# An fp32 opening for an attention and two-MoE kernel: one product in place of three for the first 24 blocks, weights split later, and gathers of 256 rows

## The chip, the cores and the metric

The kernel runs on one NeuronCore of a Trainium2 chip. The metric is the device time of one launch in microseconds (us). Five engines work beside each other, each through its own queue in order: TensorE (PE, with its weight loads shown as PEld), VectorE (DVE), ScalarE (ACT), GpSimd (POOL) and SyncE (SP), which here only issues DMAs. [...]

## The reference, cut to what matters

```python
# 1. windowed attention, 4 x 576 tokens, 8 heads of 64, window 128, ALiBi bias
scores = q @ k.T / 8 + bias            # masked to 0 <= i - j < 128
x = softmax(scores) @ v                # -> x: 2304 tokens x 512
# 2. one dense MLP, d_ff 2048; its weights are float64
h = x @ w_in;  g = where(h > 0, h, exp(min(h, 0)) - 1);  x = g @ w_out
# 3. token routing: skip score, argmax over 8 experts, then per expert (d_ff 1024)
y = gate * (relu(x @ w1[e]) @ w2[e]);  out = x + y     # where x @ w_skip > 0
```

## The kernel before, in words

**Chunks and blocks.** The 2304 tokens go in nine chunks of 256. The dense MLP of a chunk is 16 blocks of 128 hidden columns: `P1` computes `h` for a block (lines 332 to 359) and `P2` (line 361) adds the block's share to the two output accumulators `acc`. A list `seq` (line 488) sets the order of blocks: chunk 0's blocks 0 to 7, chunk 1's 0 to 7, chunk 0's 8 to 15, chunk 1's 8 to 15, and from place 32 on chunk 2 to 8 whole. "Step `st`" below is a place in that list; P2 follows its P1 by two steps. So the weights of a half of the MLP serve two chunks before the other half is needed.

**Precision.** [...] Each operand is split into a high part (ACT copies it to fp32r) and a low part (a subtraction on DVE or POOL), and three products stand for one: P1 of a block is 12 matmuls of 256 columns, P2 is 6 of 512. The first 16 heads (`NATIVE = 2` chunks, functions `n_S` to `n_xT`) are done in plain fp32 instead, with no split; a plain fp32 matmul shows as two records in the trace. The later heads (`att_A`, `att_B`, `att_C`) are split.

**The opening** is written out by hand in lines 523 to 600: a loop over `k`, in which the instructions of PE, ACT, DVE and POOL keep the program's order. In step `k` head `k` of the first 16 is done; from `k = S0 = 10` on, step `st = k - 10` of `seq` joins. The same loop converts the 32 float64 weight tiles of the MLP (a "half" is one of the two tiles of a block; `CV` says how many per `k`) to fp32 by three integer operations on DVE: `shift` writes `wt`, `top` and `low` write `wr`. Then `cut` makes the split: ACT writes the high part of `w`, POOL (first 24) or DVE (last 8) subtracts. POOL also does the subtraction of `P1_g` while `k < 26`.

**After the loop** a scheduler orders the instructions. Heads 16 to 71 come one per step or one per two steps; the routing of a chunk follows its last P2; the third part runs expert by expert (`M1`, `M2`), where `gather` reads the tokens of an expert, `xpose` transposes them on PE, and `xcut` splits them. An expert's place holds `CAP = 192` rows, read as 128 and 64 (`NJ`). Between the last dense block and the first expert, `old_rows` (line 698) brings expert 0's earlier tokens into PSUM by a product with the identity, and the rank of the last chunk's tokens (`rt_rank`) follows it on PE.

Of the kernel before, what the change touches and what calls it, by code (L numbers as in the profile page):

```python
# [28 lines left out]
NATIVE = 2  # L29
HALF = NF1 // 2  # L30
S0 = 10
PINNED = 16
GPOOL = 26
# [27 lines left out]
def attn_moe_kernel(ctx: ExitStack, tc: tile.TileContext, a, out: bass.AP):  # L61
# [43 lines left out]
    later = []  # L105
# [21 lines left out]
    def low(f, x):  # L127
        lo, hi = (W[f][x][:, :, z] for z in range(2))
        DVE.scalar_tensor_tensor(out=lo, in0=lo, scalar=29, in1=hi, op0=ALU.logical_shift_right, op1=ALU.bitwise_or)

    def cut(f, x):
        w = wp.tile([128, 2, 512], F32R, name="w", tag="w")
        v = W[f][x][:, :, 0].bitcast(F32)
        ACT.activation(out=w[:, 0], in_=v, func=ACTF.Copy)
        W[f][x] = w
        rest = lambda: (POOL if f < LO_POOL else DVE).tensor_tensor(out=w[:, 1], in0=v, in1=w[:, 0].bitcast(F32), op=ALU.subtract)
        if f < LO_POOL:
            rest()
        else:
            later.append(rest)  # L140
# [71 lines left out]
    def n_max(i):  # L212
        u, h = divmod(i, 2)
        c, hp = divmod(u, 4)
        S = St.pop(i)
        p = p_p.tile([128, 2, 256], F32, name="p")
        m = smp.tile([128, 2], F32, name="m")
        den = smp.tile([128, 2], F32, name="den")
        for t in range(2):
            lo = 128 if (c == 0 and t == 0) else 0  # L220
            DVE.tensor_tensor_reduce(out=p[:, t, lo:], in0=S[:, t, lo:], in1=bias[:, 2 * hp + h, lo:], scale=-0.125, scalar=3e38, op0=ALU.add, op1=ALU.min, accum_out=m[:, t:t + 1])
        for t in range(2):
            lo = 128 if (c == 0 and t == 0) else 0
            ACT.activation(out=p[:, t, lo:], in_=p[:, t, lo:], func=ACTF.Exp, bias=m[:, t:t + 1], scale=-1.0, accum_out=den[:, t:t + 1])
        Pt[i] = p, den

    def n_norm(i):
# [31 lines left out]
    def n_xT(i):  # L259
# [101 lines left out]
    def P2(c, f):  # L361
# [112 lines left out]
    def init_slots():  # L474
# [7 lines left out]
        for j0, n in NJ:  # L482
            nc.sync.dma_start(out=xv[j0:j0 + n], in_=zero[0:n, None, :].to_broadcast([n, NE, RW]))
# [25 lines left out]
    rq = []  # L509
    load_bias = lambda h: nc.sync.dma_start(out=bias[:, h:h + 2].rearrange("p h n -> p (h n)"), in_=a["bias"][:, h * 256:h * 256 + 512])  # L510
# [15 lines left out]
    plan = [[todo.pop(0) for _ in range(min(n, len(todo)))] for n in CV]  # L526
    for k in range(S0 + PINNED):
# [14 lines left out]
        halves = plan[k]  # L542
        if st >= 8:
            for z in halves:
                shift(*z)
        if st >= 1:
            P1_g(*seq[st - 1], POOL if k < GPOOL else DVE)
# [10 lines left out]
        if 0 <= k - 1 < 16:
            n_T(k - 1)
        if 0 <= st < 8:  # L560
            for z in halves:
                shift(*z)
        if st < 0:
            for z in halves:
                top(*z)
        if k < 16:
            n_norm(k)
        if st >= 0:
            for z in halves[0:1]:
                top(*z)  # L570
            while later:
                later.pop()()
        else:
            for z in halves:
                low(*z)
            if st < -1:
                for z in plan[k + 1]:
                    shift(*z)
        if 0 <= k - 2 < 16:
            n_xT(k - 2)  # L580
        if st >= 0:
            for z in halves[1:2]:
                top(*z)
            for z in halves:
                low(*z)
# [5 lines left out]
        for z in halves:  # L591
            if st < 0:
                later.append(lambda z=z: cut(*z))
            else:
                cut(*z)
    while later:
        later.pop()()
# [4 lines left out]
    for i in range(16, 24):  # L602
        begin[i] = i + 5, i + 5
# [25 lines left out]
    sC = {b[1]: i - 1 for i, b in begin.items() if i > 16}  # L629
    sC[begin[NU - 1][1] + 2] = NU - 1  # L630
    for st in range(PINNED, len(seq) + 2):
        if st == PINNED:
            load_h(18)
            load_h(19)
        if st == PINNED:
            for e in (PE, ACT, DVE, POOL):
                e.on = True
            split_h(16)
            split_v(8)
            split_h(17)  # L640
            for e in (PE, ACT, DVE, POOL):
                e.on = False
# [23 lines left out]
        after_P2(*seq[st - 2])  # L666
        if st in sB:
# [255 lines left out]
```

## Time and profile before

| | us |
|---|---|
| median of 3 runs | 793.34 (792.83 to 795.66) |
| the profiled execution | 792.31 |
| its span | 790.6 |
| PE busy | 737.1 (93%) |
| DVE busy | 602.3 (76%) |
| ACT busy | 534.0 (68%) |
| POOL busy | 335.6 (42%) |

The profiled execution is a run of its own, 1.03 us under the median; the 1.7 us beside its span is launch and end. Busy shares are means over stages that have different limits, so they are read by stage. In a line of the timeline the first two numbers are start and duration; `x12` counts records merged into one line; the bracket at the end is how long the engine sat idle before and what ended that.

### The profile page before, as it was taken

To read this page: it belongs to the slowest core of one execution; us is meant where nothing else is said; L and a number is where in the kernel's file an instruction comes from. 1 tells how busy PE (TensorE), PEld (TensorE's weight loads), DVE (VectorE), ACT (ScalarE), POOL (GpSimd) and SP (SyncE) were. 2 spreads that over 40 slices of the span, in tenths; PEclk is the share of its full clock that TensorE was granted. 3 is DMA by queue.
4 is the path that set the end of the run, shared out by engine and by line. 5 is a ranking of instruction groups with operands and counts; after the bars stand their busy time and mean duration, and the time that the engine had idled before them with its cause. 6 is when DMAs were issued, how large, how long until landed. Compare 5 with 4: busy or idle time off the path is not lost.

```text
span 790.6 us, 14785 instructions
## 1 busy us (share of the span) xinstructions
PE 737.1 (93%) x4963; PEld 655.1 (83%) x4965; DVE 602.3 (76%) x1563; ACT 534.0 (68%) x1416; POOL 335.6 (42%) x350
## 2 busy tenths in 40 slices
PE   6786799989999999999999999999998999999995
PEld 3364587879999989999999999999887999998894
DVE  5999994898888888888888888875335777776772
ACT  6776466777778768778777777766444766666661
POOL 1445654344454354354344344321104565655651
PEclk9889999999999999999999999999998999999998
DMA  8866117432222222222222222105014666666630
GB/s 284 310 231 230 60 50 221 125 98 93 84 62 83 86 89 61 81 71 75 80 77 88 73 76 82 34 13 211 19 47 124 216 225 218 212 208 220 232 129 29
DMA packets 43212, 98.94 MB, mean 125 GB/s; under 512 B 7779, under 2 KB 15843, under 8 KB 43132
## 3 DMA queue, kind: packets, MB, share of 16 engines
q1 hardware_dynamic: 40092, 93.40, 36.9%
q0 software_dynamic: 3040, 4.56, 1.6%
q8 instruction: 40, 0.66, 0.3%
q14 instruction: 40, 0.33, 0.1%
HBM read 85.35 MB, written 15.93 MB: 128 GB/s over the span
## 4 chain that ended last, share of the span: by engine, by line
PE 70%; DVE 16%; ACT 5%; issue 4%; DMA 3%; SPq 0%; POOL 0%; POOLq 0%; ACTq 0%; DVEq 0%
PE h L52 23%; PE acc L52 21%; PE h L744 4%; DVE wr L52 4%; DVE wt L52 3%; PE PT L52 3%; PE S L52 3%; PE PV L52 3%; PE m L52 3%; PE acc L762 2%; ACT p L52 2%; DMA w2r<-in_w2c_dram 2%; PE h L745 2%; DVE p L52 2%; DVE den L52 2%
## 5 line engine op out<-in xcount | busy, mean ns | idle before, releaser
L52 PE MATMUL h<-xT,w 128*128 128x256 f32 x1728 | 238.6, 287 | 4.8 <-DVE e L52 2.4
L52 PEld LDWEIGHTS h<-xT,w 128*128 128x128 f32 x1728 | 221.7, 191 | 12.6 <-DVE e L52 4.7
L52 PE MATMUL acc<-w,gt 128*128 128x512 f32 x864 | 225.9, 396 | 2.2 <-POOL gt L52 2.2
L52 PEld LDWEIGHTS acc<-w,gt 128*128 128x128 f32 x864 | 154.2, 191 | 28.0 <-POOL gt L52 2.6
L52 POOL TENSOR_TENSOR w<-w2r,w 128x512 fp32r<-128x512 f32 x64 | 88.3, 1400 | 86.9 <-ACT w L52 66.0
L185 POOL TENSOR_TENSOR hi<-qkr,hi 64x256 fp32r<-64x256 f32 x56 | 41.5, 741 | 166.5 <-issue 127.0
L52 ACT ACTIVATE e<-h 128x256 f32<-128x256 f32 x144 | 55.0, 382 | 75.8 <-PE h L52 75.5
L52 DVE TENSOR_TENSOR gt<-e,gt 128x256 fp32r<-128x256 f32 x129 | 59.9, 464 | 36.5 <-ACT gt L52 35.2
L52 DVE SCALAR_TENSOR_TENSOR e<-h,e 128x256 f32<-128x256 f32 x144 | 60.6, 421 | 31.0 <-ACT e L52 30.8
L52 ACT ACTIVATE p<-p,m 128x256 f32<-128x256 f32 (+1 forms) x144 | 70.5, 490 | 13.2 <-DVE m L52 12.6
L744 PE MATMUL h<-xT,w 128*128 128x384 f32 x256 | 78.7, 364 | 0.4 <-DVE xT L736 0.4
L52 ACT ACTIVATE w<-w2r 128x512 fp32r<-128x512 f32 x128 | 74.6, 628 | 5.3 <-DMA w2r<-in_w2c_dram 5.2
L52 ACT ACTIVATE gt<-e 128x256 fp32r<-128x256 f32 x144 | 58.8, 408 | 23.5 <-DVE e L52 23.1
L186 POOL TENSOR_TENSOR kl<-qkr,hi 128x384 fp32r<-128x384 f32 x56 | 62.7, 1119 | 4.4
L745 PE MATMUL h<-xT,w 128*128 128x192 f32 x256 | 64.1, 250 | 0.0
L52 ACT ACTIVATE e<-e 128x256 f32<-128x256 f32 x144 | 60.1, 417 | 4.1
L52 PE MATMUL PT<-ident,p 128*128 128x128 f32 x280 | 48.2, 289 | 14.1 <-ACT p L52 9.4
L52 POOL TENSOR_TENSOR w<-wr,w 128x512 fp32r<-128x512 f32 x24 | 35.7, 1504 | 54.0 <-ACT w L52 51.2
L52 DVE TENSOR_TENSOR w<-w2r,w 128x512 fp32r<-128x512 f32 x64 | 53.0, 865 | 6.7 <-ACT w L52 6.7
L52 PEld LDWEIGHTS PT<-ident,p 128*128 128x128 f32 x280 | 32.6, 144 | 28.7 <-ACT p L52 16.0
L52 DVE CUSTOM_DVE_ANT_0 p<-S,bias 128x256 f32<-128x256 f32 (+1 forms) x104 | 41.2, 408 | 17.0 <-PE S L52 16.9
L762 PE MATMUL acc<-gt,w 128*128 128x384 f32 x128 | 42.7, 367 | 8.3 <-DVE yT L770 5.9
(130 smaller groups left out, 1468.3 us busy)
## 6 DMA issues: line engine op xcount, KB each, us to landing
w2r<-in_w2c_dram SPq DMA_DIRECT2D x64, 512.0 KB, 4.3
qkr<-in_qk_dram SPq DMA_DIRECT2D x112, 160.0 KB, 2.9
wr<-in_w1c_dram SPq DMA_DIRECT2D x32, 512.0 KB, 6.2
v<-in_v_dram SPq DMA_DIRECT2D x36, 192.0 KB, 2.8
out_dram<-x SPq DMA_DIRECT2D x18, 256.0 KB, 3.2
qkr<-in_qk_dram SPq DMA_DIRECT2D x8, 320.0 KB, 6.0
bsp<-in_bsp_dram SPq DMA_DIRECT2D x20, 128.0 KB, 2.1
xg<-xs SPq DMA_DIRECT2D x9, 257.0 KB, 3.9
```

The costliest lines, as they stand in the source:

```text
L52: i = op(*args, **kw)
L185: eng.tensor_tensor(out=hi[64:128, 0:256], in0=r[64:128, 0:256], in1=hi[64:128, 0:256].bitcast(F32), op=ALU.subtract)
L186: eng.tensor_tensor(out=kl, in0=r[:, 256:640], in1=hi[:, 256:640].bitcast(F32), op=ALU.subtract)
L744: nc.tensor.matmul(out=h[:, 0:2 * CAP], lhsT=w[0][:, 0, kc * 128:kc * 128 + 128], rhs=x[:, kc].rearrange("p a n -> p (a n)"), start=kc == ...
L745: nc.tensor.matmul(out=h[:, 0:CAP], lhsT=w[0][:, 1, kc * 128:kc * 128 + 128], rhs=x[:, kc, 0], start=False, stop=kc == 3)
L762: nc.tensor.matmul(out=o[:, 0:2 * CAP], lhsT=w[1][:, 0, dc * 128:dc * 128 + 128], rhs=gt.rearrange("p a n -> p (a n)"), start=f == 0, stop ...
```

## The change

The constants move the loop's start of the MLP one step forward (`S0` 10 to 9), raise `NATIVE` to 3 chunks and spread the conversions differently (`CV`). `plain` names the 24 blocks (all 16 of chunk 0 and the first 8 of chunk 1) that are computed in plain fp32: P1 with 4 matmuls, P2 with 2, and `P1_g` writes `gt` in one DVE operation. `low` now writes the fp32 weights packed into the first half of their own tile, and no split follows in the loop. The splits (`parts`, 16 of them, each two ACT copies and two DVE subtractions) are handed to the scheduler at steps 16 to 27. `xf`, an unsplit x for chunks 0 and 1, takes one of the two buffers of `xTp`; `x_parts` splits chunk 1's later.

```diff
-NATIVE = 2
+NATIVE = 3
-S0 = 10
+S0 = 9
-GPOOL = 26
-CV = [0] * 2 + [1] * 8 + [2] * 8 + [1] * 8
-LO_POOL = 12
+CV = [0] * 2 + [1] * 7 + [2, 1] * 4 + [2] * 6 + [1] + [0] * 4
+C2 = 21
...
     def low(f, x):
-        lo, hi = (W[f][x][:, :, z] for z in range(2))
-        DVE.scalar_tensor_tensor(out=lo, in0=lo, scalar=29, in1=hi, op0=ALU.logical_shift_right, op1=ALU.bitwise_or)
-
-    def cut(f, x):
-        w = wp.tile([128, 2, 512], F32R, name="w", tag="w")
-        v = W[f][x][:, :, 0].bitcast(F32)
-        ACT.activation(out=w[:, 0], in_=v, func=ACTF.Copy)
-        W[f][x] = w
-        rest = lambda: (POOL if f < LO_POOL else DVE).tensor_tensor(out=w[:, 1], in0=v, in1=w[:, 0].bitcast(F32), op=ALU.subtract)
...
+        r = W[f][x]
+        v = r.rearrange("p n two -> p (n two)")[:, 0:512]
+        DVE.scalar_tensor_tensor(out=v, in0=r[:, :, 0], scalar=29, in1=r[:, :, 1], op0=ALU.logical_shift_right, op1=ALU.bitwise_or)
+        W[f][x] = v.bitcast(F32)
+
+    def parts(f):
+        for x in range(2):
+            w = wp.tile([128, 2, 512], F32R, name="w", tag="w")
+            v = W[f][x]
+            ACT.activation(out=w[:, 0], in_=v, func=ACTF.Copy)
+            DVE.tensor_tensor(out=w[:, 1], in0=v, in1=w[:, 0].bitcast(F32), op=ALU.subtract)
+            W[f][x] = w
...
+    plain = lambda c, f: c == 0 or c == 1 and f < HALF
...
+            if plain(c, f):
+                PE.matmul(out=h[:, 0:256], lhsT=w[0][:, kc * 128:kc * 128 + 128], rhs=xf[:, c, kc], start=kc == 0, stop=kc == 3)
+                continue
...
+        if plain(c, f):
+            DVE.scalar_tensor_tensor(out=gt[:, 0], in0=h[:, 0:256], scalar=0.0, in1=e, op0=ALU.max, op1=ALU.subtract)
+            G[c, f] = gt
+            return
...
+            if plain(c, f):
+                PE.matmul(out=o, lhsT=gt[:, 0, sl], rhs=w[1], start=first, stop=final)
+                continue
...
-        for j0, n in NJ:
-            nc.sync.dma_start(out=xv[j0:j0 + n], in_=zero[0:n, None, :].to_broadcast([n, NE, RW]))
+        for j0 in (0, 128):
+            nc.sync.dma_start(out=xv[j0:j0 + 128], in_=zero[:, None, :].to_broadcast([128, NE, RW]))
...
+    ready = {}
+    for f in range(HALF):
+        ready.setdefault(16 + 2 * f // 3, []).append(f)
+        ready.setdefault(20 + f, []).append(HALF + f)
...
-        for j, (j0, n) in enumerate(NJ):
-            r0 = e * TS + j0
-            nc.sync.dma_start(out=xg[e][0:n, j], in_=xs[r0:r0 + n, :])
+        nc.sync.dma_start(out=xg[e], in_=xs[e * TS:e * TS + 256, :].rearrange("(j p) w -> p j w", p=128))
...
+        for f in ready.get(st, ()):
+            parts(f)
+        if st in (18, 19):
+            x_parts(1, st - 18)
...
-        for j, (j0, n) in enumerate(NJ):
-            PE.matmul(out=pg[kc // 2][:, kc % 2, j0:j0 + n], lhsT=early[0:n, j, kc * 128:kc * 128 + 128], rhs=ident[0:n, 0:n], start=kc % 2 == 0 and j == 0, stop=False)
+        for j in range(2):
+            PE.matmul(out=pg[kc // 2][:, kc % 2, j * 128:j * 128 + 128], lhsT=early[:, j, kc * 128:kc * 128 + 128], rhs=ident, start=kc % 2 == 0 and j == 0, stop=False)
...
-                for j, (j0, n) in enumerate(NJ):
-                    nc.tensor.transpose(ps[half][:, k, j0:j0 + n], xg[e][0:n, j, kc * 128:kc * 128 + 128], ident[0:n, 0:n])
+                for j in range(2):
+                    nc.tensor.transpose(ps[half][:, k, j * 128:j * 128 + 128], xg[e][:, j, kc * 128:kc * 128 + 128], ident)
```

Heads 16 to 23 (chunk 2) run through the same `n_` functions as the first 16, one per step from step 21 (`C2`), with their loads; their probabilities are scaled on DVE, not on ACT. POOL is left without arithmetic until the split of head 24.

How the order moves shows at three places. On PE, in two steps of the loop where heads 12 to 15 are still going, this stands before (`h` is P1, `acc` is P2, `S`, `PT` and `PV` belong to a head):

```order
L52 MATMUL h<-xT,w 128x256 x12
L52 MATMUL acc<-w,gt 128x512 x6
L52 MATMUL PV<-ptn,v 64x256 x2
L52 MATMUL PV<-ptn,v 64x128 x4
L52 MATMUL PT<-ident,p 128x128 x4
L52 MATMUL h<-xT,w 128x256 x12
L52 MATMUL acc<-w,gt 128x512 x6
L52 MATMUL S<-qkr 128x256 x4
```

and this now:

```order
L51 MATMUL S<-qkr 128x256 x4
L51 MATMUL h<-xT,wr 128x256 x4
L51 MATMUL PT<-ident,p 128x128 x4
L51 MATMUL acc<-wr,gt 128x512 x2
L51 MATMUL h<-xT,wr 128x256 x4
L51 MATMUL PT<-ident,p 128x128 x4
L51 MATMUL PV<-ptn,v 64x256 x2
L51 MATMUL PV<-ptn,v 64x128 x4
L51 MATMUL acc<-wr,gt 128x512 x2
```

P1 of a block now stands ahead of the step's transpose `PT` and of `PV`, reads the unsplit `wr`, and takes 4 and 2 instructions where it took 12 and 6. On DVE, some steps after the last of the first 16 heads, two steps were before:

```order
L52 SCALAR_TENSOR_TENSOR e<-h,e 128x256
L52 SCALAR_TENSOR_TENSOR wr<-wr,wt 128x512
L52 TENSOR_TENSOR w<-wr,w 128x512
L52 SCALAR_TENSOR_TENSOR wr<-wr 128x512
L52 TENSOR_SCALAR wt<-wr 128x512
L52 SCALAR_TENSOR_TENSOR e<-h,e 128x256
L52 SCALAR_TENSOR_TENSOR wr<-wr,wt 128x512
L52 TENSOR_TENSOR w<-wr,w 128x512
```

and one step with the start of the next is now:

```order
L51 SCALAR_TENSOR_TENSOR gt<-h,e 128x256
L51 SCALAR_TENSOR_TENSOR wr<-wr,wt 128x512
L51 TENSOR_TENSOR w<-wr,w 128x512
L51 SCALAR_TENSOR_TENSOR wr<-wr 128x512
L51 SCALAR_TENSOR_TENSOR wr<-wr,wt 128x512
L51 TENSOR_TENSOR w<-wr,w 128x512
L51 SCALAR_TENSOR_TENSOR wr<-wr 128x512
L51 TENSOR_SCALAR wt<-wr 128x512 x2
L51 SCALAR_TENSOR_TENSOR gt<-h,e 128x256
```

Two halves are converted per step where one was, and the scheduler has put subtractions of the weight split (`w<-wr,w`) between them. On PE in the third part, the transposes of one expert's tokens were

```order
L728 MATMUL ps<-ident,xg 128x128
L728 MATMUL ps<-ident,xg 128x64
L728 MATMUL ps<-ident,xg 128x128
L728 MATMUL ps<-ident,xg 128x64
L728 MATMUL ps<-ident,xg 128x128
```

and so on to eight; now they are one run of `128x128 x8`, all of one shape.

## Rows read from the trace of the kernel before

**Rows 1.** Stretches: PE, PEld, DVE, ACT, POOL busy (instructions), PEclk, DMA share, GB/s.

```profile
0.00:38.70 38.70, 26.27 (x122) 13.44 (x124) 29.23 (x88) 26.09 (x80) 9.98 (x13) 0.91 0.89 300
38.70:99.40 60.70, 44.48 (x263) 33.87 (x262) 57.10 (x104) 38.46 (x98) 34.54 (x28) 0.92 0.51 175
116.40:190.00 73.60, 67.76 (x457) 58.60 (x456) 56.76 (x166) 54.62 (x149) 30.83 (x40) 1.00 0.45 133
190.00:585.00 395.00, 394.84 (x2779) 360.05 (x2777) 303.92 (x898) 282.59 (x760) 146.48 (x180) 1.00 0.25 75
603.00:771.00 168.00, 159.53 (x1077) 151.22 (x1078) 125.58 (x239) 113.35 (x287) 99.90 (x76) 1.00 0.63 208
50.00:55.00 5.00, 5.00 (x20) 4.60 (x21) 4.41 (x11) 4.00 (x12) 1.97 (x2) 0.50 0.79 257
```

**Rows 2.** The conversion on DVE: count, duration ns min/median/max, first and last start.

```profile
L52 DVE TENSOR_SCALAR wt<-wr x32: 411/877/1537, 9.9 to 115.6; 128x512 int32<-128x512 int32 x32
L52 DVE SCALAR_TENSOR_TENSOR wr<-wr,wt x32: 671/682/1785, 10.8 to 116.3; 128x512 int32<-128x512 int32 x32
L52 DVE SCALAR_TENSOR_TENSOR wr<-wr x32: 671/686/1817, 11.9 to 117.5; 128x512 int32<-128x512 int32 x32
```

**Rows 3.** Timeline of DVE and POOL in the opening.

```profile
10.28 0.28 DVE L52 CUSTOM_DVE_ANT_0 p<-S,bias 128x128 f32<-128x128 f32 x1
12.84 0.28 DVE L52 CUSTOM_DVE_ANT_0 p<-S,bias 128x128 f32<-128x128 f32 x1
...
18.84 1.52 POOL L52 TENSOR_TENSOR w<-wr,w 128x512 fp32r<-128x512 f32 x1 [2.55 <-ACT w L52]
19.12 1.52 DVE L52 TENSOR_SCALAR wt<-wr 128x512 int32<-128x512 int32 x1
...
36.09 0.41 DVE L52 CUSTOM_DVE_ANT_0 p<-S,bias 128x256 f32<-128x256 f32 x1
```

**Rows 4.** Timeline of PE in the opening, then two pieces of the chain of waits.

```profile
21.32 1.40 PE L52 MATMUL S<-qkr 64*128 64x128 f32 x8 [0.79 <-DMA qkr<-in_qk_dram]
39.72 1.67 PE L52 MATMUL h<-xT,w 128*128 128x256 f32 x12
61.12 1.13 PE L52 MATMUL S<-qkr 64*128 64x256 f32 x8
189.98 1.68 PE L52 MATMUL h<-xT,w 128*128 128x256 f32 x12
...
127.04 1.43 PE h L52 x12
128.48 1.39 PE acc L52 x6
```

**Rows 5.** Timeline of PE: fp32 records of 256 columns, then of 128.

```profile
56.24 0.39 PE L52 MATMUL PV<-ptn,v 128*64 128x256 f32 x2
56.46 0.39 PE L52 MATMUL PV<-ptn,v 128*64 128x128 f32 x4
```

**Rows 6.** Timeline of PE and DVE: an expert's transposes, transposes alike, the old rows.

```profile
617.20 1.86 PE L728 MATMUL ps<-ident,xg 128*128 128x128 f32 x8
...
589.79 0.66 PE L52 MATMUL m<-ident,x 128*128 128x128 f32 x4
...
594.04 3.33 PE L52 MATMUL h<-ident,xg 128*128 128x128 f32 x12
597.30 0.22 PE L52 MATMUL m<-oh,tri 128*128 128x8 bf16 x2
...
595.19 0.18 DVE L52 TENSOR_TENSOR oh<-k,actv 128x16 bf16<-128x16 f32 x1
```

**Rows 7.** The weight split and the end of P1: durations, and a page line.

```profile
L52 ACT ACTIVATE w<-wr x32: 638/675/713, 14.1 to 118.7; 128x512 fp32r<-128x512 f32 x32
L52 DVE TENSOR_TENSOR w<-wr,w x8: 675/679/1226, 98.7 to 119.4; 128x512 fp32r<-128x512 f32 x8
L52 DVE SCALAR_TENSOR_TENSOR e<-h,e 128x256 f32<-128x256 f32 x144 | 60.6, 421 | 31.0 <-ACT e L52 30.8
```

More of the change, by code (lines that the diff above doesn't have):

```diff
@@ L104, in attn_moe_kernel @@
     W = {}
-    later = []
     T, rawv, vsp = {}, {}, {}
@@ L170, in load_v, with load_special @@
         rawv[u] = v
+        if not native(2 * u):
+            load_special(u)
+    def load_special(u):
+        c, hp = divmod(u, 4)
         for t in range(2):
@@ L220, in n_max @@
             lo = 128 if (c == 0 and t == 0) else 0
-            DVE.tensor_tensor_reduce(out=p[:, t, lo:], in0=S[:, t, lo:], in1=bias[:, 2 * hp + h, lo:], scale=-0.125, scalar=3e38, op0=ALU.add, op1=ALU.min, accum_out=m[:, t:t + 1])
+            b = bsp[u, t][:, h] if (c, t) in SPECIAL else bias[:, 2 * hp + h]
+            DVE.tensor_tensor_reduce(out=p[:, t, lo:], in0=S[:, t, lo:], in1=b[:, lo:], scale=-0.125, scalar=3e38, op0=ALU.add, op1=ALU.min, accum_out=m[:, t:t + 1])
         for t in range(2):
@@ L233, in n_norm @@
             lo = 128 if (c == 0 and t == 0) else 0
-            ACT.activation(out=p[:, t, lo:], in_=p[:, t, lo:], func=ACTF.Copy, scale=den[:, t:t + 1])
+            if c < 2:
+                ACT.activation(out=p[:, t, lo:], in_=p[:, t, lo:], func=ACTF.Copy, scale=den[:, t:t + 1])
+            else:
+                DVE.tensor_scalar(out=p[:, t], in0=p[:, t], scalar1=den[:, t:t + 1], scalar2=None, op0=ALU.mult)
         Pt[i] = p
@@ L263, in n_xT, with x_parts @@
             return
-        if i % 8 == 1:
+        if i % 8 == 1 and c > 0:
             xT[c] = xTp.tile([128, 2, 4, 256], F32R, name="xT")
-        x_split(xT[c], hp, PVt.pop(u))
+        if c < 2:
+            ACT.activation(out=xf[:, c, hp, :], in_=PVt.pop(u), func=ACTF.Copy)
+        else:
+            x_split(xT[c], hp, PVt.pop(u))
         rawv.pop(u)
+    def x_parts(c, j):
+        x, v, ks = xT[c], xf[:, c], slice(2 * j, 2 * j + 2)
+        ACT.activation(out=x[:, 0, ks], in_=v[:, ks], func=ACTF.Copy)
+        DVE.tensor_tensor(out=x[:, 1, ks], in0=v[:, ks], in1=x[:, 0, ks].bitcast(F32), op=ALU.subtract)
     def x_split(xt, hp, x):
@@ L525, in attn_moe_kernel @@
     todo = [divmod(n, 2) for n in range(2 * NF1)]
-    plan = [[todo.pop(0) for _ in range(min(n, len(todo)))] for n in CV]
+    plan = [[todo.pop(0) for _ in range(n)] for n in CV]
     for k in range(S0 + PINNED):
@@ L541, in attn_moe_kernel @@
             nc.sync.dma_start(out=t, in_=src)
[L542 to L545, printed above, removed]
         if st >= 1:
-            P1_g(*seq[st - 1], POOL if k < GPOOL else DVE)
+            P1_g(*seq[st - 1], DVE)
         if k < 16:
@@ L550, in attn_moe_kernel @@
             n_max(k)
-        if st < 0:
-            while later:
-                later.pop()()
         if k < len(WK):
             warm(WK[k], 512)
+        fresh = k - 2 in (7, 15)
+        if st >= 0 and not fresh:
+            P1_mm(*seq[st])
+            P1_exp(*seq[st])
+        if 0 <= k - 1 < 16:
+            n_T(k - 1)
+        for z in plan[k][0:1]:
+            top(*z)
+            low(*z)
+        if k < 16:
+            n_norm(k)
+        for z in plan[k][1:2]:
+            top(*z)
+            low(*z)
         if 0 <= k - 2 < 16:
             n_PV(k - 2)
[L558 to L579, printed above, removed]
-            n_xT(k - 2)
[L581 to L585, printed above, removed]
+            n_xT(k - 2)
+        if fresh:
             P1_mm(*seq[st])
@@ L590, in attn_moe_kernel @@
             after_P2(*seq[st - 2])
[L591 to L597, printed above, removed]
+        for z in plan[k + 1]:
+            shift(*z)
     P1_g(*seq[PINNED - 1], DVE)
@@ L628, in attn_moe_kernel @@
     sB = {b[1]: i for i, b in begin.items()}
-    sC = {b[1]: i - 1 for i, b in begin.items() if i > 16}
+    sC = {b[1]: i - 1 for i, b in begin.items() if i > 24}
     sC[begin[NU - 1][1] + 2] = NU - 1
     for st in range(PINNED, len(seq) + 2):
[L632 to L642, printed above, removed]
+        k = st - C2 + 16
+        if k in (14, 16, 18, 20):
+            load_pair(k // 2 + 1)
+            load_v(k // 2 + 1)
+        if k == 22:
+            load_v(12)
+            load_h(24)
+            load_h(25)
+        if k == 23:
+            split_h(24)
+            split_v(12)
+            split_h(25)
+            load_v(13)
+            load_h(26)
+            load_h(27)
         if st == PINNED:
```

32 lines of the change are left out of this document (18 added, 14 removed).

## The prediction

> **What bounds the kernel now.** I read the busy time by stretches first [rows 1]. From 190 to 585 us PE is busy 394.84 of 395.00: nothing but PE's own work counts there, and this change leaves that work alone. In the third part, 603 to 771, PE is busy 159.53 of 168.00, so PE time saved there is nearly all time saved. The opening is another matter: from 38.7 to 99.4 DVE is busy 57.10 of 60.70 while PE idles 16 us, and before 38.7 the DMA engines are 89% busy at 300 GB/s. From 116.4 to 190 PE idles another 5.8 us. So the question is when PE reaches the saturated stretch. As mark I take P1 of step 33 (the second block of chunk 2), which starts at 189.98; from there both kernels have the same PE queue up to 585.
>
> Then the groups by line say why DVE is slow. A conversion is a `wt` and two `wr` instructions: at best 0.41 + 0.67 + 0.67, at worst 1.54, 1.79 and 1.82 [rows 2]. The timeline shows the reason: POOL's weight subtraction runs from 18.84 for 1.52 us, and the `wt` of DVE that starts at 19.12 ends with it, also after 1.52 [rows 3]. Where POOL did nothing, a step of the loop took 12.84 - 10.28 = 2.56; from 12.84 to 36.09, six steps, 3.88 each.
>
> **The change part by part.**
>
> *Before the first block.* Conversions lose POOL, so a step should fall back to 2.56 wherever data are there. Up to S of heads 6 and 7 they are not: PE waits for the q/k load until 21.32 [rows 4], and the loads ahead of it are the same now. A pair of heads with two halves is 320 + 192 + 2 x 512 KB = 1.57 MB, at 300 GB/s 5.2 us for two steps, which is DVE's pace too. So the softmax of head 9 starts at 21.32 + 0.3 + 3 x 2.6 = 29.4 instead of 36.09 [rows 3]. The first P1 followed it by 39.72 - 36.09 = 3.6, and does so again (its x waits for the same chain, one step earlier in the loop): 33.0 instead of 39.72. Ends: 30.5 (the loads come sooner, since POOL no longer holds anything) and 36 (a step of 3.6, as with POOL).
>
> *The fp32 blocks on PE.* The trace has no plain P1 or P2, but it has plain fp32 records. Those of PV go two abreast, in two column halves; a pair of 256 columns starts at 56.24 and the next pair at 56.46 [rows 5], so 0.22 a record, and a plain matmul is two records. P1 becomes 4 x 2 x 0.22 = 1.76 against 1.43 now [rows 4]; P2, 2 x 2 records of 512 columns, is also 1.76 against 1.39. That is 0.70 more per block, 16.8 for 24. Ends: no more than now (0), and 0.28 a record, from the S group's 1.13 for four in a row [rows 4], 2.26 a piece and 40.8 in all; that row holds the first load and the tail, so I stay with the spacing of starts.
>
> *The heads.* Heads 16 to 23 in plain fp32 cost PE per pair an S group of 1.13, two transposes and a PV (2 records of 256 and 4 of 128 columns in a row, 0.88), against four score matmuls and four value matmuls a head now: even within 1 us in all. They spare ACT and POOL the q, k and v splits.
>
> *PE from the first P1 to step 33.* 24 plain blocks 84.5; 9 split P1 at 1.43 and 7 split P2 at 1.39, 22.6; 7 S groups at 1.13, 7.9; 15 transpose groups at 0.66 [rows 6], 9.9; 8 PV at 1.0, 8.0; two split heads and the first routing, about 5 (the same instructions as before). Sum 138, less some 3 for tails that the next instruction covers (0.1 in each of 30 groups): 135.
>
> *What PE waits for on the way.* From steps 18 to 23 DVE has two conversions a step, the end of P1 (0.42) and about one subtraction of the weight split (0.68) [rows 7]: 3.5 + 0.42 + 0.68 = 4.6 by durations, 4.2 by starts (the 2.56 step holds 2.79 of durations). PE needs 3.52, so DVE is late by 0.7 in six steps, 4 us. The eight late heads wait at 0.5 each, as the ten there did in 5.8 us of idle from 116.4 to 190: another 4. So 135 + 8 = 143, and step 33 starts at 33 + 143 = 176, 14 us sooner. Without the 16.8 us of fp32 passes it would be 31. Ends: no waits, 22 sooner; the waits of before (8% of idle plus the 16 us), 5 later.
>
> [...]
>
> *The weight split, moved.* 32 ACT copies (0.68) and 32 DVE subtractions (0.68) [rows 7], 22 us on each engine. Some nine stand in steps 18 to 24 and are counted above. The others lie from step 15 on, where a step has 3.5 or more of PE and DVE needs 0.42 + 2.7 x 0.68 = 2.3: hidden. If that cover is gone, the first rival is what happens. Of the other edits, the fill of the expert slots (2 x 128 x 8 rows of 2056 bytes, 4.2 MB, 14 us at 300 GB/s, a quarter more than now) goes out on SP at step 20, ahead of the loads of heads 20 and 21, which are due at step 25, five steps or 17 us later; the gather is one issue for 256 rows instead of two. Both at nothing; 3 us if these loads come late.
>
> *The tail.* An expert's eight transposes alternate between 128 and 64 rows and take 1.86; four alike take 0.66, so eight alike 0.66 + 4 x 0.11 = 1.10 [rows 5, 6]. Seven experts: 5.3 us. Ends: 0 (PE waits for something else then) and 7 us. The old rows likewise: 12 records, half of them of 64 rows, run from 594.04 to 597.30, and the rank of the last chunk starts only then, although DVE had its input at 595.19 + 0.18 [rows 6]. Twelve alike at 0.11 end near 595.4, so the rank follows 1.9 sooner; ends 0 and 2.5.
>
> *Sum:* -14 - 5.3 - 1.9 = -21.2. The profiled execution took 792.31, so 771.1; its runs' median is 1.03 higher, so 772 as a median.
>
> **The rivals.**
>
> 1. *The split holds DVE and ACT.* There are 33 weight buffers and 32 hold raw weights, so each copy has to wait for the subtraction before it: 32 links of 0.68 + 0.68 = 44 us in series. From step 18 (near 75 us) to the first use at step 24 (near 135) there is room, but both queues are in order, and a copy that waits holds back the exponentials of P1 behind it. If 0.4 us of each link shows, 13 of the 14 us in the opening go: 785. For it: DVE has 57 of 61 us in the opening now [rows 1]. Against it: in steps 16 to 20 little else stands on DVE.
>
> 2. *The third part does not follow.* If the weights' DMA and POOL's split (POOL 99.90 of 168.00, DMA share 0.63 [rows 1]) set the pace there, the shorter transposes become waits: 5.3 less, 777. Against it: PE idles only 8.5 us in 168.
>
> 3. *The clock makes it slower.* PE's work in fp32 until step 8 is about 40 us, from 33 to 73. If it stays at the lower clock, as from 50 to 55, it takes twice that: 40 - 21 = 19 us slower, 811. It decides from 21 us of PE work at half clock on. For it: the stretch just named. Against it: 38.7 to 99.4 has 0.92 although PE idled 16 us, and there is less idling now. [...]
>
> 4. *PE hardly waits* and the loads are early: 8 + 2.5 us more, 762.
>
> 5. *POOL was not what slowed DVE*, so the change does not do what it seems to: then a step stays at 3.88, the first P1 comes at 37, and the fp32 passes add 16.8 to a bound that DVE keeps; no change or a loss of a few us. The 0.41 against 1.52 in [rows 2, 3] leaves almost nothing for it.
>
> **How the numbers follow.** Forecast 0.65, rival 1 0.12, rival 2 0.10, rival 3 0.04, rival 4 0.07, rival 5 0.02. A change under 0.5% (4 us) could not be told from none here. Faster by more: the forecast, rivals 2 and 4 and most of rival 1, 0.91. Within 0.5%: the rest of rival 1 and half of rival 5, 0.04. Slower: 0.05. The likeliest case alone has 765 to 781 (waits of 2 to 15 us); to hold 8 in 10 the range takes in rival 2, most of rival 4 and the near half of rival 1: 762 to 785.
>
> **What would show it.** Right: `wt` at 0.41 throughout the opening; the first P1 near 33; a plain P1 start to start 1.76; step 33 near 176; PE at full share from there, with the same length to the end of the dense part; eight transposes in 1.1; the rank within 0.1 us of its input. Wrong: P1 records spaced by more than 0.22, a granted clock well under 1 after 40 us, DVE waiting for ACT `w` in rows from step 16 on, or expert lengths still at 22 us.

## The result, and the profile after

The change takes the median from 794.48 us (792.83 to 795.66, 4 runs) to **773.82 us** (772.30 to 774.66, 4 runs): a ratio of 0.9736, 95% interval 0.9711 to 0.9762. The profiled execution took 774.66, span 772.8. The forecast was 772.

Stretches first, as in [rows 1]: busy time of PE, PEld, DVE, ACT, POOL, then TensorE's granted clock as a share of its full speed, DMA share, GB/s.

```profile
0.00:36.40 36.40, 26.09 (x114) 13.37 (x116) 22.40 (x87) 22.09 (x71) 0.45 (x6) 0.76 0.80 277
36.40:100.00 63.60, 63.28 (x281) 42.36 (x280) 54.85 (x132) 37.28 (x95) 0.88 (x5) 0.98 0.62 215
100.00:176.35 76.35, 75.09 (x427) 55.10 (x425) 49.74 (x154) 52.21 (x137) 8.61 (x12) 1.00 0.35 114
176.35:572.75 396.40, 395.70 (x2782) 360.44 (x2780) 305.98 (x898) 282.75 (x761) 148.05 (x183) 1.00 0.26 77
586.65:755.00 168.35, 156.59 (x1086) 152.67 (x1087) 131.88 (x240) 111.47 (x288) 101.60 (x79) 0.98 0.66 216
```

From the first P1 on PE now idles 0.3 us up to 100 and 1.3 us from there to step 33, where it idled 16 and 6 before. The conversions, against [rows 2] (count, ns min/median/max, first and last start):

```profile
L51 DVE TENSOR_SCALAR wt<-wr x32: 400/418/427, 9.3 to 97.7; 128x512 int32<-128x512 int32 x32
L51 DVE SCALAR_TENSOR_TENSOR wr<-wr,wt x32: 671/686/696, 11.0 to 98.4; 128x512 int32<-128x512 int32 x32
L51 DVE SCALAR_TENSOR_TENSOR wr<-wr x32: 682/693/695, 11.7 to 99.6; 128x512 int32<-128x512 int32 x32
```

Not one of them is stretched any more; the 96 instructions of the conversion take DVE 56.4 us, where they took 81.2. The timeline of PE shows the first P1 and that of step 33, against [rows 4]; the last two lines are pieces of the chain of waits (start, duration), a plain P2 and a plain P1.

```profile
36.42 3.54 PE L51 MATMUL h<-xT,wr 128*128 128x256 f32 x8
...
176.35 1.68 PE L51 MATMUL h<-xT,w 128*128 128x256 f32 x12
```

```profile
62.18 1.72 PE acc L51 x4
63.90 1.73 PE h L51 x8
```

The first block took 3.5 us, twice the 1.73 of the later P1: the granted clock was 0.56 from 36.42 to 39.96 and 1.00 from 62 to 66. The tail, against [rows 6]: old rows, rank, select products (the 16 products that pick the last chunk's tokens for the first expert) and an expert's transposes on PE.

```profile
581.41 1.60 PE L51 MATMUL h<-ident,xg 128*128 128x128 f32 x12
582.85 0.20 PE L51 MATMUL m<-oh,tri 128*128 128x8 bf16 x2
...
584.36 2.04 PE L51 MATMUL h<-gt,w 128*128 128x192 f32 x16
...
605.63 1.04 PE L747 MATMUL ps<-ident,xg 128*128 128x128 f32 x8
```

The old rows of before, 3.33 us in [rows 6], had run at a granted clock of 0.66 (the column behind the five engines), which the prediction did not look up; the new ones ran at 1.00.

```profile
594.00:597.30 3.30, 3.30 (x13) 2.40 (x14) 1.60 (x11) 0.22 (x1) 0.00 (x0) 0.66 0.00 0
```

And one thing is new. POOL, DVE and PE in the first expert:

```profile
588.62 0.97 POOL L494 DMA_INDIRECT tb<-x,sloti  x1 [0.30 <-PE h L764]
589.62 4.94 POOL L51 TENSOR_TENSOR w<-w2r,w 128x512 fp32r<-128x512 f32 x4
```

```profile
589.31 6.42 DVE L51 TENSOR_TENSOR w<-w2r,w 128x512 fp32r<-128x512 f32 x2 [0.16 <-ACT w L51]
595.64 0.34 DVE L770 SCALAR_TENSOR_TENSOR gt<-e,gt 128x192 fp32r<-128x192 f32 x1
```

```profile
596.04 0.69 PE L781 MATMUL acc<-gt,w 128*128 128x384 f32 x1 [5.38 <-DVE gt L770]
```

POOL has two blocks of expert weights waiting behind its four scatters and does their four subtractions in a row (a "row of four" below). DVE's two subtractions, 1.3 us elsewhere, take 6.4 and end 1.2 after POOL's; the `gt` behind them comes late and PE waits 5.4 us.

The account by marks, with a second profiled execution of the same kernel (from the experiments) beside the first:

| stretch, us | before | forecast | after | again |
|---|---|---|---|---|
| first P1 starts | 39.72 | 33.0 | 36.42 | 33.65 |
| from there to step 33 | 150.26 | 143 | 139.93 | 138.91 |
| step 33 to the last P2 of the second part | 395.43 | same | 396.43 | 395.25 |
| from there to the first M1 | 17.59 | 15.7 | 13.90 | 13.89 |
| first M1 to the next expert's transposes | 14.20 | same | 18.95 | 19.04 |
| from there to the end of the span | 173.4 | 168.1 | 167.2 | 167.2 |

### The profile page after: what moved, and what is told of

It reads as the page before. It is cut to its first block, busy times and chain, and to the rows that moved or that the text cites. A ratio compares the mean times of both kernels' runs of the same rounds, so it can differ in the third digit from the quotient of the medians.

```text
span 772.8 us, 14285 instructions
## 1 busy us (share of the span) xinstructions
PE 738.5 (96%) x4835; PEld 642.5 (83%) x4837; DVE 577.1 (75%) x1548; ACT 514.1 (67%) x1370; POOL 263.1 (34%) x287
## 4 chain that ended last, share of the span: by engine, by line
PE 75%; DVE 12%; ACT 5%; issue 4%; DMA 3%; POOL 1%; SPq 0%; POOLq 0%; ACTq 0%
PE h L51 25%; PE acc L51 23%; PE PV L51 4%; PE S L51 4%; PE PT L51 4%; DVE w L51 4%; PE h L763 3%; PE m L51 3%; PE acc L781 2%; DVE gt L770 2%; ACT w L51 2%; DVE wr L51 2%; DVE p L51 2%; DMA qkr<-in_qk_dram 2%; PE h L764 1%
## 5 line engine op out<-in xcount | busy, mean ns | idle before, releaser
L51 PE MATMUL h<-xT,w 128*128 128x256 f32 x1440 | 197.7, 287 | 0.0
L51 PEld LDWEIGHTS h<-xT,w 128*128 128x128 f32 x1440 | 183.2, 190 | 5.5 <-issue 1.0
L51 PE MATMUL acc<-w,gt 128*128 128x512 f32 x720 | 186.1, 394 | 0.0
L51 PEld LDWEIGHTS acc<-w,gt 128*128 128x128 f32 x720 | 127.2, 189 | 21.9 <-issue 0.9
L187 POOL TENSOR_TENSOR hi<-qkr,hi 64x256 fp32r<-64x256 f32 x48 | 35.4, 738 | 199.0 <-issue 98.9
L51 DVE TENSOR_TENSOR gt<-e,gt 128x256 fp32r<-128x256 f32 x120 | 55.7, 464 | 34.3 <-ACT gt L51 33.0
L51 ACT ACTIVATE p<-p,m 128x256 f32<-128x256 f32 (+1 forms) x144 | 70.4, 489 | 10.3 <-DVE m L51 10.0
L51 DVE SCALAR_TENSOR_TENSOR e<-h,e 128x256 f32<-128x256 f32 x120 | 50.6, 422 | 31.1 <-ACT e L51 30.9
L51 ACT ACTIVATE gt<-e 128x256 fp32r<-128x256 f32 x120 | 48.9, 407 | 23.4 <-DVE e L51 23.1
L188 POOL TENSOR_TENSOR kl<-qkr,hi 128x384 fp32r<-128x384 f32 x48 | 54.0, 1125 | 3.8
L770 DVE SCALAR_TENSOR_TENSOR gt<-e,gt 128x192 fp32r<-128x192 f32 x64 | 41.3, 645 | 15.6 <-ACT gt L769 15.6
```

Of the source, the lines that this page charges most:

```text
L51: i = op(*args, **kw)
L187: eng.tensor_tensor(out=hi[64:128, 0:256], in0=r[64:128, 0:256], in1=hi[64:128, 0:256].bitcast(F32), op=ALU.subtract)
L188: eng.tensor_tensor(out=kl, in0=r[:, 256:640], in1=hi[:, 256:640].bitcast(F32), op=ALU.subtract)
L770: nc.vector.scalar_tensor_tensor(out=gt[:, 1], in0=hc, scalar=0.0, in1=gt[:, 0].bitcast(F32), op0=ALU.max, op1=ALU.subtract)
```

## The experiments

**The changed kernel again.** No edit.

> The changed kernel once more, unaltered, for a second profile beside the two variants. Theory (what the opening's first P1 and the clock there do differs from execution to execution of one kernel): 772 to 775, first P1 anywhere from 33 to 36.5, the row of four POOL subtractions and a PE wait of 5 us in the first expert again. Rival (they are fixed by the order of work): first P1 within 0.3 of 36.4 and a clock near 0.50 from 20 to 34.

773.25 (769.63 to 778.22), ratio 0.9749 (0.9720 to 0.9777). Two lines of its PE timeline, and the stretch from 20 to 34 here and then in the first profile of this kernel:

```profile
33.65 2.53 PE L51 MATMUL h<-xT,wr 128*128 128x256 f32 x8
...
172.56 1.68 PE L51 MATMUL h<-xT,w 128*128 128x256 f32 x12
```

```profile
20.00:34.00 14.00, 10.16 (x58) 5.65 (x58) 12.06 (x42) 10.12 (x33) 0.00 (x0) 0.78 0.83 287
```

```profile
20.00:34.00 14.00, 10.73 (x46) 5.70 (x46) 9.27 (x33) 8.34 (x28) 0.00 (x0) 0.50 0.76 257
```

The same instructions start their first P1 at 36.4 in one execution and 33.7 in the next; from there to step 33 both take 139 to 140. The granted clock differs with it: 0.50 in every 2 us of that stretch, against 0.78 on average; in both PE waits there for ACT's `p`, 1.9 and 2.4 us at the longest. Over the seven profiles here whose instructions are the same up to the first P1 it lies from 33.3 to 36.4, at clocks of 0.50 to 0.82; the order is not strict (35.1 at 0.82, 33.3 at 0.76), so how much of the spread the clock makes is not shown. The row of four and a PE wait of 5.3 us are there again.

**POOL's arithmetic moved to DVE**, in the kernel before.

```diff
-GPOOL = 26
-LO_POOL = 12
+GPOOL = 0
+LO_POOL = 0
```

> The kernel before with POOL's arithmetic in the opening given to DVE (24 subtractions of 128x512 and 15 of 128x256), nothing else changed: blocks stay split. Theory (POOL's work at the same time is what stretched DVE's conversions): every conversion falls from 4.9 to 1.75 us, for 0.69 more per subtraction, so that DVE needs 2.6 + 0.7 a step ahead of the first block and loses its excess of 57 us busy in 61 after it: first P1 near 36 to 37, step 33 near 176 to 182, 780 to 787. Rival (POOL is not the cause, the conversions are slow by themselves): DVE gets 24 x 0.69 + 15 x 0.43 = 23 us more, 805 to 817. Rival (the gain of the opening needs the subtractions gone from it, that is plain fp32): 790 to 796.

803.20 (799.54 to 805.11), ratio 1.0126 (1.0101 to 1.0151): slower by 1.3%. Its `wt`, a wait of DVE up to 100 us, and its first P1:

```profile
L52 DVE TENSOR_SCALAR wt<-wr x32: 405/421/424, 9.4 to 123.8; 128x512 int32<-128x512 int32 x32
```

```profile
DVE w L52 <- ACT w L52: 10.0, 8, 1.4
```

```profile
45.80 1.42 PE L52 MATMUL h<-xT,w 128*128 128x256 f32 x5
```

The first half of the theory holds: without POOL no conversion is stretched, and all of them together take DVE 55.9 us instead of 81.2. Its time is wrong, by over 16 us. The added subtractions stand in DVE's queue behind ACT's copies and DVE waits for those, so the first P1 comes 6 us later than before. Relieving POOL is not enough where DVE gets the subtractions. None of the three times I gave was right; the nearest was the rival that counts DVE's added work, 805 to 817.

**POOL arithmetic put back, for nothing**, in the changed kernel.

```diff
+        if f < 12:
+            POOL.tensor_tensor(out=scr[0], in0=W[f][x], in1=scr[0].bitcast(F32), op=ALU.subtract)
...
```

(with the scratch tile `scr[0]`, which is chunk 1's split x before it is written)

> The changed kernel plus idle arithmetic on POOL in the opening: each of the first 24 converted weight halves is also subtracted on POOL into a scratch tile that nothing reads before it is overwritten; DVE, ACT and PE have the same work. It is the test that giving the subtractions to DVE could not be, since DVE then waited for ACT's copies. Theory (POOL's arithmetic stretches DVE's): the wt and wr beside a POOL subtraction go from 0.41 and 0.68 to 1.5 and 1.8, some 1.3 us per half; of 24 x 1.3 = 31 us about a third lies in DVE's waits ahead of the first P1, so that the first P1 comes 2 to 4 later and step 33 some 5 to 15 later: 779 to 789. Rival (DVE's time was lost to something else that the change removed): 773 to 775.

783.75 (781.19 to 786.73), ratio 0.9838 (0.9807 to 0.9870): 10 us of the 21 are gone by the medians, 8 by the ratios. But ACT once waits 6.8 us for the scratch tile, so I made the test smaller (`f < 9`, 18 halves for 24):

> As the run with idle POOL arithmetic in the opening, for the first 18 weight halves instead of 24, so that POOL is done before ACT overwrites the scratch tile (in that run ACT waited 6.8 us for POOL there, which POOL's effect on DVE has no part in). Theory (DVE is stretched): the loss shrinks with the halves and without that wait, but stays: wt beside POOL at 1.5, no wait of ACT for POOL, 776 to 781. Rival (the 10 us lost were that wait): 772.5 to 775.

777.54 (777.39 to 777.72), ratio 0.9787 (0.9725 to 0.9849). POOL and DVE there, then the first P1 and that of step 33:

```profile
19.71 1.27 POOL L51 TENSOR_TENSOR xT<-wr,xT 128x512 fp32r<-128x512 f32 x1 [2.29 <-DVE den L51]
```

```profile
19.78 1.49 DVE L51 TENSOR_SCALAR wt<-wr 128x512 int32<-128x512 int32 x1
```

```profile
37.37 3.21 PE L51 MATMUL h<-xT,wr 128*128 128x256 f32 x8
...
179.08 1.68 PE L51 MATMUL h<-xT,w 128*128 128x256 f32 x12
```

DVE's `wt`, 0.42 alone, starts 0.07 after POOL's subtraction and ends 0.29 after it, with not one instruction of DVE added. By the medians 3.7 us are lost (the interval touches that of the changed kernel); a wait of ACT for the scratch tile is left, 2.5 us, so not all of it is the stretching. The size stays between 0 and 10 us; the stretching is seen in each pair of rows. But little of the gain goes with it. The conversions take 72.8 us of DVE here and 78.9 with 24 halves, so two thirds and nine tenths of the 24.8 us that the change took from them are back; yet step 33 comes at 179.08 and 184.67, still 10.9 and 5.3 sooner than before, where the changed kernel has 13.6 and 17.4 in its two profiles.

**The gathers alone**, in the kernel before, and **the gathers undone**, in the changed kernel.

```diff
-        for j, (j0, n) in enumerate(NJ):
-            r0 = e * TS + j0
-            nc.sync.dma_start(out=xg[e][0:n, j], in_=xs[r0:r0 + n, :])
+        nc.sync.dma_start(out=xg[e], in_=xs[e * TS:e * TS + 256, :].rearrange("(j p) w -> p j w", p=128))
```

(with the slots' fill, old rows and transposes that belong to it)

> The kernel before with one part of the change alone: gathers of 256 rows, so that each expert's eight transposes and the twelve products of the old rows are all of 128 rows. Theory (the transposes carry what the third part gained, and the new stall of the first expert comes from its first M1 starting sooner against POOL's four scatters): seven times 0.8 us for the transposes, 1.9 for the old rows, up to 1.8 more if the clock then stays up at the select products, less 4.75 minus the 2.1 that PE waited there already; 794.5 - 5.7 - 1.9 (to 3.7) + 2.7 = 788 to 790, with PE waiting some 5 us for a gt near the third product of the first expert. Rival (the stall comes from how the opening's split leaves the weight buffers): no stall, 785 to 787. Rival (the transposes become waits in the third part): 792 to 793.

> The changed kernel with that one part undone: gathers in pieces of 128 and 64 rows. Theory: transposes back to 1.86 (+5.7), old rows and the lower clock behind them back (+1.9 to +3.7), the stall in the first expert back to its 2.1 us (-2.7): 773.8 + 5 to 7 = 779 to 781; the opening stays as it is, step 33 at 176.4. Rival (the stall comes from the opening's part): it stays, 781.5 to 783.5. Rival (the clock that stays up in the third part comes from the opening): the select products stay at 2.0 us and the end of the dense part does not grow by more than 1.9.

Alone: 788.41 (786.27 to 789.41), ratio 0.9931 (0.9911 to 0.9951), as the theory had it. Undone: 776.78 (773.28 to 782.42), ratio 0.9804 (0.9767 to 0.9842), 2 us less than the theory: neither the stall nor the clock went back. The clock that stays up is what the second rival had, but it holds with the old opening too (select products 2.04 with the gathers alone). Both have the row of four; POOL with the gathers alone, and old rows, select products and PE's wait with the gathers undone:

```profile
601.49 4.95 POOL L52 TENSOR_TENSOR w<-w2r,w 128x512 fp32r<-128x512 f32 x4
```

```profile
577.93 2.41 PE L51 MATMUL h<-ident,xg 128*128 128x128 f32 x12
...
581.73 2.04 PE L51 MATMUL h<-gt,w 128*128 128x192 f32 x16
```

```profile
PE acc L783 <- DVE gt L772: 5.3, 1, 5.3
```

So the stall needs neither the new opening (it comes with the old one too) nor the new gathers (it comes without them). In the profile of before the select products ran partly at half clock (2.99 us for 16, granted 0.65 on average), and the first M1 came late enough that POOL's two blocks came apart, at 604.04 and 607.28, and DVE got in between. PE then waited 2.1 us. With POOL's arithmetic moved to DVE, where the select products took 2.62, the blocks came apart by 0.2 us and PE waited 3.6. Where the clock holds (2.04), M1 meets the row of four. The shorter old rows are worth 2.41 - 1.60 = 0.8 where the clock held (select products 2.04 in both); the rest of the 3.7 saved ahead of M1 is clock (0.50 from 597.3 to 600 before, 1.00 from 581.4 to 586.4 now). Why it held with the gathers undone, in the same instructions that lost it in the profile of before, stays open. The profiles only show that it held in all eleven with old rows of one shape, and in one of three with the old rows of two shapes.

**Blocks 3 and 5 on DVE**, in the changed kernel.

```diff
-            split(w, r[:, x], POOL if n % 2 else DVE)
+            split(w, r[:, x], POOL if n % 2 and n not in (3, 5) else DVE)
```

> The changed kernel with one thing more: the weight subtractions of the third part's blocks 3 and 5 run on DVE instead of POOL. Theory (four of POOL's subtractions in a row, 589.6 to 594.6, keep DVE's from running, and PE waits 5.4 us for the gt behind it): the stall goes, or leaves 1 us for DVE's four more subtractions of 0.68: 769 to 770.5. Rival (the weights of these blocks are late, or DVE is too full there): no gain, 773 to 775.

770.06 (769.55 to 771.19), ratio 0.9707 (0.9688 to 0.9726): in the range of the theory, but a second wait took the first one's place, and the profiled execution (769.55) had some luck: its first P1 came at 33.3, the earliest of all. Waits in the first expert, then SP's queue:

```profile
ACT w L51 <- DMA w2r<-in_w2c_dram: 5.9, 1, 5.9
...
PE acc L781 <- DVE gt L770: 4.5, 2, 4.0
```

```profile
583.92 1.40 SPq L611 DMA_DIRECT2D xg<-xs  x3
585.70 24.73 SPq L615 DMA_DIRECT2D w2r<-in_w2c_dram  x10
```

The load of block 7 goes out behind three gathers of 0.5 MB; ACT's copy of it waits 5.9 us, with the relu behind it.

**More blocks ahead.** `AHEAD = 5` for 3.

> The changed kernel with five of the third part's blocks converted in the second part instead of three (AHEAD 5): POOL's subtractions of block 3 then stand ahead of its last scatters, and the load of block 7 no longer queues behind three gathers. Theory (the first expert waits first for POOL's four subtractions in a row, and where these are gone for that load, 585.7 to 595.0 in the run with blocks 3 and 5 on DVE): neither wait is left, PE runs the first expert in 14.2 us or less from its first M1 to the first transpose, 768.5 to 770 (with the run above at 770.1). Rival (the work moved into the second part makes PE wait there, DVE has 0.85 of 2.82 a step): 771 to 774.

772.80 (771.01 to 774.12), ratio 0.9708 (0.9683 to 0.9732), not told apart from the changed kernel. POOL:

```profile
588.23 4.94 POOL L51 TENSOR_TENSOR w<-w2r,w 128x512 fp32r<-128x512 f32 x4
```

So the rival's time came (771 to 774), for another reason: my expectation overlooked that the loop's own blocks move along: 5 and 7 instead of 3 and 5, both odd, both on POOL. The stall is unchanged, as its cause says it must be.

**Blocks 3 and 5 on DVE, and the two later gathers issued behind the load.**

```diff
-    gather(1)
...
-        if f == GF and e + 2 < NE:
-            gather(e + 2)
+        if st == 3 or f == GF and e + 2 < NE:
+            with tc.issue_after(fetched[-1]):
+                gather(1 if st == 3 else e + 2)
```

(with the list `fetched` of the loads that belongs to it, and the edit of blocks 3 and 5 above)

> The changed kernel with the weight subtractions of the third part's blocks 3 and 5 on DVE, and the gathers for the second and third expert issued behind the load of block 7 instead of ahead of it. Theory (once POOL's row of four is gone the first expert waits for that load, which stood behind three gathers: issued at 585.7, there at 595.0): load 3 to 4 us sooner, the 4.0 us wait of the run with blocks 3 and 5 on DVE shrinks to 1 or less, from the first M1 to the first transposes 14 us: 1.5 to 4 below the changed kernel with these blocks on DVE alone (770.1), 766 to 768.5. Rival (the transposes of the second expert now wait for its later gather): 770 to 773.

769.18 (768.10 to 769.82), ratio 0.9680 (0.9657 to 0.9704), against 0.9749 (0.9720 to 0.9777) for the changed kernel on the same chip: about 4 us better by the medians, with its first P1 at 36.2. Against blocks 3 and 5 alone it is 0.9 by the medians, and the intervals overlap: what the later gathers add is not told apart. From the first M1 to the transposes it takes 597.70 - 584.56 = 13.1, as hoped; but the next expert takes 23.7 where the later ones take 21.2 to 21.5, and the median lies 0.7 above what I expected. There POOL has four subtractions in a row again. POOL, and the wait of PE from 586 to 610:

```profile
601.23 6.10 POOL L51 TENSOR_TENSOR w<-w2r,w 128x512 fp32r<-128x512 f32 x4 [3.66 <-ACT w L51]
```

```profile
PE acc L781 <- DVE gt L770: 2.6, 3, 1.8
```

**Fillers for the clock**, on top of that.

```diff
-WK = 1, 3, 3, 3, 1, 1, 1, 1, 1
+WK = 1, 3, 3, 3, 3, 3, 3, 3, 3
```

> As the run beside it (blocks 3 and 5 on DVE, gathers behind the load), with three filler matmuls instead of one in steps 4 to 8, ahead of the first P1. Theory (the profiled runs of one and the same opening have their first P1 at 33.3 to 36.4, with granted clocks of 0.50 to 0.82 from 20 to 34, and where the first P1 was late its block ran at half clock: the clock costs up to 3 us there): a clock of 0.9 or more from 20 to 45, first P1 at 32.5 to 34, 1 to 2.5 below its neighbour. Rival (the fillers stand in the chain of the softmax on PE, 2 x 0.22 us a step): 0 to 2 above its neighbour. Rival (the spread comes from the loads): no change.

**767.33** (766.56 to 769.12), ratio 0.9662 (0.9638 to 0.9687), the best here. Without the fillers, then with them:

```profile
20.00:34.00 14.00, 9.77 (x46) 5.37 (x46) 9.44 (x34) 8.55 (x28) 0.00 (x0) 0.63 0.77 277
34.00:45.00 11.00, 11.00 (x60) 7.84 (x61) 8.83 (x29) 7.93 (x25) 0.00 (x0) 0.85 0.81 281
```

```profile
20.00:34.00 14.00, 10.67 (x65) 5.80 (x66) 12.61 (x45) 11.15 (x37) 0.00 (x0) 0.87 0.80 274
34.00:45.00 11.00, 11.00 (x61) 7.78 (x58) 8.77 (x28) 8.43 (x24) 0.00 (x0) 0.94 0.93 342
```

The clock is higher, though 0.87 up to 34 where I expected 0.9, and the first P1 comes at 34.5 instead of 36.2, half a microsecond outside what I expected. The step of 1.9 by medians is what the theory gave, but the intervals overlap and the spread of the opening is as large: likely, not shown.

**The softmax's reciprocal ahead of the conversion.**

```diff
+        if k < 16 and st < 0:
+            n_norm(k)
         for z in plan[k][0:1]:
...
-        if k < 16:
+        if k < 16 and st >= 0:
             n_norm(k)
```

> The changed kernel with one reorder ahead of the first block: DVE works out the softmax's reciprocal before it converts the weight half of that step, no longer behind it. Theory (ahead of the first P1 the pace is a loop of two steps: scores, maximum, exponential, reciprocal, scaling, transposes, and the next scores queued behind them on PE; a conversion of 1.4 us lies in it): the scores of a pair come 5.3 to 6.0 us after those of the pair before instead of 6.1 to 6.9, the first P1 1 to 3 us sooner than at the same granted clock, 771 to 773. Rival (the loads, held on SP behind the v buffer, or DVE itself set the pace): no change, 773.5 to 775.

775.43 (772.27 to 777.24), ratio 0.9745 (0.9717 to 0.9772): no change. Waits up to 40 us:

```profile
DVE den L51 <- ACT p L51: 7.3, 9, 1.3
PE S L51 <- DMA qkr<-in_qk_dram: 6.5, 3, 3.9
```

DVE waits for the exponentials instead, and the scores wait for their load (two of the three waits 1.3 us each): loop and loads lie close to each other, and shortening one meets the other.

**The third chunk's heads undone**, in the changed kernel: `NATIVE = 2` with the old loads, splits and order of heads 16 to 23.

> The changed kernel with the third chunk's heads 16 to 23 back in split form (q, k and v split on ACT and POOL, scores in four products, old order and old loads); the plain fp32 blocks and the gathers stay. Theory of the prediction (the plain heads cost PE the same within 1 us and spare ACT and POOL work that lies beside): 772 to 776. Rival (POOL's splits at 100 to 170 us stretch DVE's weight split there and PE waits): 777 to 782. Rival (the plain heads cost PE more than the split ones did): 769 to 772.

777.06 (776.00 to 778.67), ratio 0.9760 (0.9730 to 0.9791). By medians 3.2 to 3.8 more than the changed kernel, by intervals unclear; the median lies at the near end of the rival (POOL's splits stretch DVE's weight split), not in the theory. Its profile has 144.5 from the first P1 (34.99) to step 33 (179.49) instead of 139 to 140. PE is as busy there as in the changed kernel, 138.5 us against 138.4 and 137.3; it waits 6.0 us instead of 1.6. Below are a wait between 100 and 185 that the changed kernel has only once, for 0.5 us, and what stands ahead of the longest of the six, on POOL and on DVE:

```profile
PE PT L51 <- DVE p L51: 4.9, 6, 1.4
```

```profile
123.36 1.00 POOL L188 TENSOR_TENSOR kl<-qkr,hi 128x384 fp32r<-128x384 f32 x1
...
123.47 1.44 DVE L51 TENSOR_TENSOR w<-wr,w 128x512 fp32r<-128x512 f32 x1 [0.65 <-ACT w L51]
```

DVE's weight subtraction, 0.69 alone, takes 1.44 beside POOL's split of k, and the scaling of `p` that PE waits for stands behind it. The second longest wait shows the same (1.47 at 134.09, beside POOL's at 133.99).

## Why the prediction was right, step by step

**The cause in the opening** (POOL stretches DVE): the stretching is shown, its share of the gain is not. `wt` is at 0.41 where POOL is quiet and at 1.5 where it is put back, from 0.07 after the start of POOL's subtraction to 0.29 after its end; by what means POOL holds it up no run here shows. But with 18 halves put back 10.9 of the 13.6 to 17.4 us up to step 33 stay (5.3 with 24, where ACT also waited 6.8 for the scratch tile), and in the kernel before, handing POOL's arithmetic to DVE ended the stretching and gained nothing. So a good part of the opening's gain, over half by the smaller test, goes with what the change did besides: no split before a block can start, one DVE operation for `gt`, P1 ahead of the transposes, the loop one step sooner (`S0`). No run separates these.

**The first P1 at 33.0** (ends 30.5 to 36): 33.65 and 36.42, the one near, the other just past the end. The step I assumed, "back to 2.56 wherever data are there", is not what sets it: in the first profile DVE waits over 2 us for scores twice (1.1 and 0.5 in the second), and the scores follow each other in 5.6 to 7.0 us for two steps, where I had 5.2, through a loop over PE, DVE and ACT that runs partly at half clock (granted 0.91 from 15 to 20, 0.50 from 20 to 36.4). The sum had no term for the clock, which left a gap: the first P1 moves by up to 3 us between executions, at clocks from 0.50 to 0.82. Part of what the start gained is not POOL's: with its arithmetic put back the first P1 came at 36.9 and 37.4, against 39.7 before.

**Plain blocks at 1.76**: 1.72 and 1.73.

**135 of work and 8 of waits to step 33**: 139 to 140 in all, and only 1.6 of it idle. The waits were mis-sized. DVE does need 4.6 us a step there (in the chain of waits the pairs of split subtractions start at 85.54, 90.16 and 94.78), but conversions run ahead of the blocks, and one late P1 of 0.3 us is all that comes of it; I had multiplied the shortfall by six steps and left out the lead. PE's work was 2 to 3 larger than the sum. Both errors are small and of opposite sign: 143 against 139 to 140. Step 33 at 176: 176.35 and 172.56.

**The heads "even within 1 us in all"**: for PE's work, yes: 138.5 us with the heads undone, 138.4 and 137.3 without. What undoing them cost, 5 in the profile, is waits: 6.0 against 1.6. The prediction named what brings them ("they spare ACT and POOL the q, k and v splits") and gave it no price: POOL's splits stretch DVE's weight split, 0.82 us on average instead of 0.69.

**Transposes at 1.10, 5.3 saved**: 1.04, and 6.2 with the last expert and the tail. Eight transposes that alternate between 128 and 64 rows took 1.86 and eight alike 1.04; what makes the alternation slower no run here shows.

**Old rows, 1.9 sooner**: 0.8. The term was taken from a row that ran at a clock of 0.66, so about half of it was clock and not the shape of the old rows. In all 3.7 were saved ahead of the first M1, the rest by the clock. **And the first expert "same"**: 4.8 longer, which no step and no rival had. The two are linked. POOL's scatters follow the rank and end 6.7 us behind it before (597.30 to 604.02) and 6.7 after (582.85 to 589.59), while M1 follows the rank by 5.7 before and 3.8 after, since the clock held (3.8 also with the gathers undone, where it held too). So the 1.9 us gained between rank and M1 are waited for behind M1; the rest of the loss is the row of four and the half clock after it (0.50 from 594 to 599).

**The rivals.** 1: the chain of copies and subtractions exists (ACT waits 14.0 us for DVE's, DVE 9.4 for ACT's), but PE hardly waits for it. 2: out, the third part did follow. 3: the clock was at 0.50 to 0.78 from 20 to 34 in the two profiles, but that is mostly ahead of the first P1, where the rival had not placed it: 0.75 and more from 34 to 45, 1.00 from 45 on. 4: PE hardly waits from the first P1 on, as it had it. 5: out as far as the stretching goes.

**The sum.** By the marks after less before: -3.3 - 10.3 + 1.0 - 3.7 + 4.75 - 6.2 = -17.75 for the first profile, and -22.7 for the second, around the forecast of -21.2 and the -20.7 of the medians. The total was right with two terms missing (the spread of the start of the first block, the stall of the first expert) and two too pessimistic (waits, the end of the second part). That they nearly cancel is luck.

## What to carry to other kernels

Arithmetic on GpSimd stretched VectorE's beside it here (`wt` 1.49 us instead of 0.42), so look at the spread of one instruction's durations; but handed to VectorE it brought a wait for its input with it (10.0 us up to 100), and nothing was gained (803.20 against 794.36). Put a suspected cause back into the new kernel and see how much of the gain goes: here over half of it stayed in the smaller of two tests. Read the granted clock of a row before taking a price from it. When a stage ahead of a queue becomes faster, look at what that queue holds at the new time: here two blocks had piled up behind POOL's scatters. Profile the changed kernel twice before giving a few us of an opening to a cause.

## What the runs showed of the hardware

- Beside four POOL subtractions in a row (589.62 to 594.56) the first of DVE's two took 5.8 us, from 589.31 to 595.12, where the median of its kind is 0.69: it ended behind all four, not behind one.
- After that wait PE came back at half clock: 0.69 and 0.57 a product instead of 0.44 and 0.36, until 599.4; the granted clock was 0.50 from 594 to 599 and 1.00 from 600.
- The granted clock in the opening differs between executions of one program: 0.50 and 0.78 from 20 to 34 in two of them.
